# Block-causal attention and SwiGLU on one core: float64 weights unpacked with fewer instructions, keys turned in place, a new instruction list with more filler matmuls

## The chip, the cores and the metric

The kernel runs on one core of one Trainium2 chip. The metric is the device time of one execution in microseconds (us). TensorE (PE) multiplies matrices into PSUM, VectorE (DVE) and ScalarE (ACT) work elementwise, GpSimd (POOL) takes maxima and sums over partitions here, and SyncE (SP) issues nearly all DMAs.

## What is computed

```python
def _attn_ref(q, k, v):                      # (8 batches, 8 heads, 576 positions, 64)
    scores = np.matmul(q, k.transpose(0, 1, 3, 2)) / np.sqrt(64)
    mask = block_i >= block_j                # blocks of 64 positions
    scores = np.where(mask, scores, -1e9)
    scores = scores - scores.max(-1, keepdims=True)
    attn = np.exp(scores)
    attn = attn / (attn.sum(-1, keepdims=True) + 1e-9)
    return np.matmul(attn, v)

def _moe_ref(x, w_gate, w_val, w_out):       # x: (4608, 512), from all heads; weights 512 x 1536, 1536 x 512
    g = x @ w_gate
    silu = g * (1.0 / (1.0 + np.exp(-g)))
    return (silu * (x @ w_val) @ w_out).astype(np.float32)
```

The three weight matrices arrive as float64, q, k and v as float32.

## The kernel before

**The list.** The whole kernel is written as tasks: `add(engine, cost, rank, fn, after, bufs, ...)` makes one, with an assumed cost, a rank, what it comes after and the buffers it uses. `in_order()` then plays all tasks through against their assumed costs. At each moment every engine takes, of the tasks that could run and for whose buffers there is room, the one of lowest rank. What comes out is one fixed instruction order per engine, and each engine executes its own strictly in that order. Ranks come from tables: `PIECES` and `AHEAD` (36 weight pieces), `FIRST` (attention of batches 0 and 1), `SIDE`, `LEAD`, `EAGER`. A DMA's landing is assumed as the queue's end plus 0.9 us. Times up to `SETTLED` = 215 us of that play are treated as the opening.

**Filler.** Where the play leaves PE idle for more than 0.3 us in the opening, `keep_busy` puts filler matmuls (64 columns of `ones`, result unused) in front of the next PE task: `int(gap / 0.25)` of them at the very start, `int(0.6 * gap / 0.12)` afterwards. Each filler call is two passes in the trace.

**Attention.** Heads go in pairs. For batches 0 and 1 (`plain_scores`) q and k are turned by PE (line 435), copied out of PSUM by ACT into `parts` (line 443), multiplied into `at` or `po` (line 461), copied to `sc` (479, 493); DVE takes a running maximum (729), POOL the maximum over partitions (733), DVE subtracts (757), ACT takes the exponential (761), PE multiplies by v and by `ones` (801). From batch 2 on `row_scores` turns q and k with DVE (648) and splits each into a rounded part and a rest (651, 654), so that three fp32r products (672) make up a full one. It holds the raw q and k in one buffer of the pair `qk` and the turned keys in the other.

**Weights.** Each of the 36 pieces (12 chunks of gate, val and out) is loaded as pairs of 32-bit words of a float64 (968), and made a float32: ACT writes the sign bits apart into `ob` (`signs`, 983), ACT scales the high word (`scaled`, 987), DVE shifts the low word right by 29 and ors the sign in (`fraction`, 992), DVE shifts the high word left by 3 and ors (`exponent`, 997). Then ACT rounds (`high`, 1002) and DVE takes the rest (`low`, 1005).

**Feed-forward.** Tiles of 256 tokens: `xhl` (token parts) times `g_even`, `g_odd`, `v_all` into `gv` (line 1124), tanh and products on ACT and DVE (1163 to 1179), then `hhl` times w_out into `po` (1223 to 1225). The first tiles run between the attention of batches 0 and 1, as their weights arrive; the last tiles are done in three pairs with seven products in place of eight (1498, 1619 to 1621).

The lines of the weight unpacking and of the filler before:

```python
        def signs():
            nc.scalar.mul(to, w, 2.0**-60)                     # to: 16-bit halves of y ("ob")
        def fraction():
            nc.vector.scalar_tensor_tensor(
                words_of(0), words_of(0), 29, s, ALU.logical_shift_right, ALU.bitwise_or)
    ...
        for _ in range(int(t.gap / 0.25 if t.at < 8.0 else FILL * t.gap / 0.12)):
            nc.tensor.matmul(to[0:D, 0:D], lhsT=ones, rhs=ones, start=True, stop=True)
```

Of the kernel before, what the change touches and what calls it, by code (L numbers as in the profile page):

```python
# [10 lines left out]
F16 = mybir.dt.float16  # L11
# [7 lines left out]
def kernel(  # L19
# [33 lines left out]
    LEAD, EAGER = 1.69311, 0.3  # L53
# [5 lines left out]
    ROWS = (2, 3, 4, 5, 6, 7)  # L59
# [4 lines left out]
    AHEAD = {(0, 1): 2.01, (0, 2): 2.07, (1, 0): 2.03, (1, 1): 2.5, (1, 2): 2.5}  # L64
    LATER = 0.6

    PIECES = [
        (2.46498, 1.85126, 2.0295),
        (4.86232, 5.94853, 3.63137),
        (4.59615, 2.52017, 1.48427),  # L70
        (3.86967, 3.05824, 5.34888),
        (1.93206, 3.59139, 2.41171),
        (5.13877, 6.90631, 5.83015),
        (3.57653, 2.93377, 2.93471),
        (0.0797053, 1.36382, 0.915695),
        (-2.09572, -5.85789, -4.34371),
        (-7.47749, -5.87222, -3.82425),
        (-7.64215, -9.14061, -8.44419),
        (-12.1092, -9.50108, -10.8836),
    ]  # L80

    SIDE = (2.97811, 4.18833)

    PATIENCE = 10.0
    FILL = 0.6

    FIRST = {
        0: [(0, 256, (-4.21445, 2.40818, 2.05548, 2.12375)), (256, 576, (-2.9124, -2.06995, -6.61901, -4.10645))],
        1: [(0, 256, (4.0214, 3.93624, 4.15916, 3.63076)), (256, 576, (-2.93177, 1.89587, 2.55533, 4.50202))],
# [5 lines left out]
    SETTLED = 215.0  # L95
# [97 lines left out]

    unseen = const.tile([P, 1], F32, name="unseen")
# [55 lines left out]
    def chunks_of_zero(KHL):  # L250
        nc.gpsimd.memset(KHL[:, :, S:SP].bitcast(F32), 0.0)

    def zeros(x):
        def fill(QL, KS):
            nc.vector.memset(KS[:, S:SP].bitcast(F32), 0.0)
            nc.vector.memset(QL[own(1 - x)].bitcast(F32), 0.0)

        return fill

# [7 lines left out]
        high=([([P, 2, QKW], F32R)], None),  # L267
        keys=([([P, 2, QKW], F32R)], chunks_of_zero),
# [14 lines left out]
        low0=([([P, S], F32R), ([P, SP], F32R)], zeros(0)),  # L283
        low1=([([P, S], F32R), ([P, SP], F32R)], zeros(1)),
# [8 lines left out]

    pool_of(
        const,
        "ob",
        2,
        out=([([P, DM], F32)], None),
        signs=([([P, DM, 2], F16)], lambda t: nc.gpsimd.memset(t.bitcast(F32), 0.0)),
    )  # L300
    pool_of(
        const,
        "wo",
        5,
        raw=([([P, (1 + wide) * DM], I32 if wide else F32)], None),
# [216 lines left out]

# [1342 lines left out]
```

## Time and profile before

| | us |
|---|---|
| median of 3 runs (1148.54 to 1151.68) | 1150.09 |
| the profiled execution, its own time | 1151.43 |
| its span, first to last instruction | 1149.7 |
| PE busy in the span | 1127.7 |
| DVE / ACT / POOL busy | 888.5 / 605.4 / 320.9 |

"Busy" is the time in which at least one instruction of the engine was under way. The span less PE's busy time is what PE spent idle. A filler matmul counts as busy.

### The profile page before, as it was taken

The page shows a single profiled execution, that of the slowest core. Times are in us where ns is not written, and L with a number is a line of the kernel's source. Part 1 is how long each engine was busy: PE and PEld are TensorE (multiplying, and loading weights), DVE is VectorE, ACT ScalarE, POOL GpSimd, SP SyncE. Part 2 cuts the span into 40 slices and gives each one's busy share as a digit, 9 for nine tenths or more (in the row PEclk, how much of TensorE's full clock was granted, in tenths as well). Part 3 has the DMA queues.
Part 4 walks back from the last instruction along what each step waited for, and adds up shares of the span by engine and source line. Part 5 has one row for each costly group of instructions (what it writes and reads, how often), then busy time and mean ns, then how long its engine had stood idle before and what let it go on. Part 6 is the DMA issues. An engine that isn't in the chain of part 4 may idle for free.

```text
span 1149.7 us, 22749 instructions
## 1 busy us (share of the span) xinstructions
PE 1127.7 (98%) x8728; PEld 995.9 (87%) x8728; DVE 888.5 (77%) x1526; ACT 605.4 (53%) x1126; POOL 320.9 (28%) x139
## 2 busy tenths in 40 slices
PE   7999999999999999999999999999999999999998
PEld 5677778898899898888888889888999999999997
DVE  5899898687787889989899898888753855656554
ACT  5888777565554555455565555455422433334323
POOL 3213111036643543334434535444320000000000
PEclk9999999999999999999999999999999999999999
DMA  8767757676665767876786758673468867767761
GB/s 196 192 183 186 204 167 267 171 210 182 167 158 147 203 178 206 225 220 173 206 224 186 207 159 246 175 205 119 167 235 259 272 217 235 236 229 247 234 201 69
DMA packets 294445, 228.92 MB, mean 199 GB/s; under 512 B 196608, under 2 KB 245008, under 8 KB 294336
## 3 DMA queue, kind: packets, MB, share of 16 engines
q1 hardware_dynamic: 291760, 226.75, 67.3%
q8 instruction: 68, 1.11, 0.4%
q10 hardware_dynamic: 2576, 0.72, 0.3%
q14 instruction: 41, 0.34, 0.1%
HBM read 190.45 MB, written 36.96 MB: 198 GB/s over the span
## 4 chain that ended last, share of the span: by engine, by line
PE 84%; DMA 5%; DVE 4%; ACT 4%; SPq 1%; issue 1%; POOL 0%; DVEq 0%; POOLq 0%; ACTq 0%
PE gv L1124 31%; PE gv L1498 15%; PE at L801 6%; PE at L672 6%; PE po L1223 5%; PE po L1224 5%; PE po L1225 5%; PE po L1620 1%; PE po L1619 1%; PE at L1621 1%; PE po L1621 1%; PE at L1620 1%; PE at L1619 1%; DMA wo<-in_moe_w_val_dram 1%; DMA wo<-in_moe_w_gate_dram 1%
## 5 line engine op out<-in xcount | busy, mean ns | idle before, releaser
L852 POOL PARTITION_ALL_REDUCE mx<-mx x48 | 180.1, 3799 | 212.0 <-DVE mx L729 153.8
L733 POOL PARTITION_ALL_REDUCE mx<-mx x80 | 138.3, 1778 | 309.6 <-DVE mx L729 218.9
L1124 PE MATMUL gv<-xhl,v_all 128*128 128x256 f32 x1728 | 219.3, 279 | 1.7 <-DVE v_all L1005 1.1
L1124 PEld LDWEIGHTS gv<-xhl,v_all 128*128 128x128 f32 x1728 | 206.5, 188 | 7.4 <-issue 2.8
L757 DVE TENSOR_TENSOR sc<-sc,mx 128x640 f32<-128x640 f32 (+6 forms) x168 | 123.6, 774 | 16.4 <-POOL mx L733 16.4
L761 ACT ACTIVATE sc<-sc 128x1024 f32<-128x1024 f32 (+3 forms) x104 | 106.2, 1032 | 48.0 <-DVE sc L757 47.4
L1124 PE MATMUL gv<-xhl,g_even 128*128 128x256 f32 x864 | 117.9, 281 | 0.0
L1124 PE MATMUL gv<-xhl,g_odd 128*128 128x256 f32 x864 | 116.9, 282 | 0.0
L1124 PEld LDWEIGHTS gv<-xhl,g_even 128*128 128x128 f32 x864 | 110.8, 188 | 6.9 <-issue 1.9
L729 DVE TENSOR_TENSOR mx<-mx,sc 128x128 f32<-128x128 f32 (+2 forms) x180 | 110.9, 619 | 2.1 <-ACT sc L493 0.4
L1124 PEld LDWEIGHTS gv<-xhl,g_odd 128*128 128x128 f32 x864 | 106.2, 188 | 5.1 <-issue 2.6
L1223 PE MATMUL po<-wo,hhl 128*128 128x512 f32 x252 | 101.6, 403 | 0.0
L1224 PE MATMUL po<-wo,hhl 128*128 128x512 f32 x252 | 98.7, 392 | 0.0
L1225 PE MATMUL po<-wo,hhl 128*128 128x512 f32 x252 | 98.3, 390 | 0.0
L801 PE MATMUL at<-sc,v 128*64 128x128 f32 (+4 forms) x848 | 90.0, 361 | 2.2 <-ACT parts L443 1.4
L689 ACT ACTIVATE sc<-at 128x576 f32<-128x576 f32 (+1 forms) x96 | 75.8, 835 | 27.7 <-PE at L672 27.6
L1176 ACT CAST hhl<-t 128x512 fp32r<-128x512 f32 x72 | 44.7, 621 | 82.8 <-DVE t L1171 70.8
L801 PEld LDWEIGHTS at<-sc,v 128*64 128x64 f32 x848 | 56.0, 137 | 35.8 <-ACT parts L443 1.6
L1179 DVE TENSOR_TENSOR hhl<-t,hhl 128x512 fp32r<-128x512 f32 x72 | 71.3, 990 | 17.2 <-ACT hhl L1176 17.2
L729 DVE TENSOR_TENSOR mx<-sc 128x896 f32<-128x896 f32 (+2 forms) x68 | 70.0, 1031 | 7.4 <-ACT sc L701 3.9
L672 PE MATMUL at<-parts,qk 64*128 64x288 f32 (+4 forms) x864 | 73.3, 310 | 0.7 <-ACT sc L689 0.7
L672 PEld LDWEIGHTS at<-parts,qk 64*128 64x128 f32 x864 | 62.0, 185 | 9.6 <-issue 1.1
(223 smaller groups left out, 2041.2 us busy)
## 6 DMA issues: line engine op xcount, KB each, us to landing
wo<-wo_d SPq DMA_DIRECT2D x164, 512.0 KB
v_all<-sum_d SPq DMA_DIRECT2D x36, 512.0 KB
v_all<-sum_d SPq DMA_DIRECT2D x72, 256.0 KB
sum_d<-wo SPq DMA_DIRECT2D x48, 256.0 KB
v<-in_v_dram SPq DMA_DIRECT2D x64, 128.0 KB
qk<-in_q_dram SPq DMA_DIRECT2D x112, 72.0 KB
out_dram<-ob SPq DMA_DIRECT2D x30, 256.0 KB
qk<-in_k_dram SPq DMA_DIRECT2D x104, 72.0 KB
```

The source lines that it names most:

```text
L672: nc.tensor.matmul(ps[0][:, x, o : o + w], lhsT=part(1, kl)[own(x), c * P : (c + 1) * P], rhs=part(0, ql)[own(x), qs : qs + w], start=n == ...
L729: nc.vector.tensor_tensor(into, prev, of(c), op)
L733: nc.gpsimd.partition_all_reduce(m, m, channels=P, reduce_op=bass_isa.ReduceOp.max)
L757: nc.vector.tensor_tensor(piece(c), scores_of(c), m, ALU.subtract)
L761: nc.scalar.activation(x, x, AF.Exp)
L801: nc.tensor.matmul(ps[0][own(x), 1 - i if sums else i, q0 - s0 : s1 - s0], lhsT=ones if sums else vt[0][:, 2 * lane + c, own(x)], rhs=sc[0 ...
L852: nc.gpsimd.partition_all_reduce(m, m, channels=P, reduce_op=bass_isa.ReduceOp.add)
L1124: nc.tensor.matmul(o, lhsT=hilo[a][:, d], rhs=xs[d][1][b][:, 0:w], start=ds[0] == 0 and n == 0, stop=ds[-1] == NDC - 1 and n == len(trio) - 1,
L1223: nc.tensor.matmul(po, lhsT=hi, rhs=whi, start=i + y == 0, stop=False)
L1224: nc.tensor.matmul(po, lhsT=hi, rhs=wlo, start=False, stop=False)
L1225: nc.tensor.matmul(po, lhsT=lo, rhs=whi, start=False, stop=i + y == NFC - 1)
L1498: nc.tensor.matmul(ps[0][:, half * XT : (half + 1) * XT], lhsT=stationary(a, j, s), rhs=part(o, j, m), start=begin and k == 0, stop=all(a ...
```

## The change

The source calls shrink, and nearly every table number changes; so does the place of most instructions.

- **Weights.** `signs` is gone. The sign now comes out of `scaled`, which uses `Prelu` with a slope that gives negative words another factor. `fraction` no longer ors a sign in: for the 18 pieces listed in `SHIFTED` it is a DVE shift with one input (line 876), for the other 18 an ACT instruction that reads the top byte of the low word and scales it (line 874, its bias from the tile `floor`). `ob` is no longer used for signs.
- **q and k.** Raw q and k lie in the same `qk` buffer that later takes the turned keys, so a pair of heads holds one of the two buffers, not both. The key's rounding waits for both turns. ACT now writes 64 columns of zeros behind the keys per half for each pair of heads (24 more instructions from batch 2 on); POOL wrote them once.
- **The list.** DMAs that are issued between 8 and 60 us of the play are assumed to land 1.2 or 1.5 us later. After 215 us an `at` buffer is taken as free 0.8 us later and an attention task on PE as ready 0.8 us later. All ranks are new.
- **Filler.** `FILL * gap / 0.12` with 0.6 becomes `FILL * gap / 0.06` with 0.8. The program holds 226 filler calls, 96 before; the first two groups (13 and 6) stay.
- An unused variant of the scores (`split_scores`) is deleted.

```diff
-    LEAD, EAGER = 1.69311, 0.3
+    LEAD, EAGER = 5.982852, 22.492407
...
-    AHEAD = {(0, 1): 2.01, (0, 2): 2.07, (1, 0): 2.03, (1, 1): 2.5, (1, 2): 2.5}
+    AHEAD = {(0, 1): 18.047719, (0, 2): 4.730354, (1, 0): -3.813423, (1, 1): 4.489137, (1, 2): -6.161143}
...
+    SHIFTED = ((0, 0), (1, 0), (1, 1), (1, 2), (2, 0), (3, 0), (3, 1), (3, 2), (4, 0), (4, 1), (6, 2), (7, 0), (8, 0), (8, 2), (9, 0), (9, 1), (10, 0), (10, 2))
...
-    FILL = 0.6
+    FILL = 0.8
...
+    EARLY = 60.0
+    SETTLED, MARGIN = 215.0, 0.8
...
-        def signs():
-            w = words_of(1).bitcast(F32)
-            to = y[0].rearrange("p (n m) t -> p n m t", n=parts)[:, :, :, 1]
-            nc.scalar.mul(to, w, 2.0**-60)
 
         def scaled():
             w = words_of(1).bitcast(F32)
-            nc.scalar.mul(w, w, 2.0**-112)
+            nc.scalar.activation(w, w, AF.Prelu, scale=2.0**-112, alpha=-(2.0**32))
+        by_act = (i, kind) not in SHIFTED
 
         def fraction():
-            s = y[0].rearrange("p m t -> p (m t)").bitcast(I32).rearrange("p (n m) -> p n m", n=parts)
-            nc.vector.scalar_tensor_tensor(
-                words_of(0), words_of(0), 29, s, ALU.logical_shift_right, ALU.bitwise_or
-            )
+            if by_act:
+                tops = raw[0].bitcast(U8).rearrange("p (n t) -> p n t", t=8)[:, :, 3]
+                tops = tops.rearrange("p (n m) -> p n m", n=parts)
+                nc.scalar.activation(words_of(0), tops, AF.Identity, scale=1.0 / 32, bias=floor)
+                return
+            nc.vector.tensor_scalar(words_of(0), words_of(0), 29, None, ALU.logical_shift_right)
...
+                    if i:
+                        nc.scalar.mul(keys[0][:, :, S:SP], zeros, 0.0)
...
                 if t.moves:
                     queue = max(queue, end + 0.65) + t.moves
                     done = queue + 0.9 + t.more
+                    if 8.0 < now < EARLY:
+                        done += 1.2 if t.moves < 1.2 else 1.5
...
-                    u.free_at = max(u.free_at, done)
+                    u.free_at = max(u.free_at, done + (MARGIN if u.tag == "at" and now > SETTLED else 0.0))
...
-        for _ in range(int(t.gap / 0.25 if t.at < 8.0 else FILL * t.gap / 0.12)):
+        for _ in range(int(t.gap / 0.25 if t.at < 8.0 else FILL * t.gap / 0.06)):
```

Three places show how the list moved. The first is on ACT, where the second weight piece (`wo_0_109`, of w_val) stands among the copies of the turned q and k out of PSUM. Before:

```order
L443 ACTIVATE parts_1_90<-gv_0_175 128x288
L1002 CAST g_even_75<-wo_0_108 128x4x128
L983 ACTIVATE ob_0_84<-wo_0_109 128x512
L987 ACTIVATE wo_0_109<-wo_0_109 128x512
L761 ACTIVATE sc_0_243<-sc_0_243 128x2x384
L443 ACTIVATE parts_1_87<-at_0_203 128x576
L355 CAST xhl_0_92<-xt_0_311 128x256
```

and now:

```order
L647 ACTIVATE sc_0_245<-sc_0_245 128x2x384
L427 ACTIVATE parts_0_86<-at_0_199 128x384
L874 ACTIVATE wo_0_109<-wo_0_109,floor 128x512
L427 ACTIVATE parts_1_87<-at_0_199 128x576
L866 ACTIVATE wo_0_109<-wo_0_109 128x512
L339 CAST xhl_0_92<-xt_0_305 128x256
```

Before, three instructions stood between the arrival of the weight and the copy of 576 columns (983, 987, 761); now one does (874), and the exponential has moved ahead of it.

The second is on PE, at the scores of the second tile of batch 0 (line 461 before, 445 now; lines 1836 and 1720 are the filler). Before:

```order
L461 MATMUL at_0_203<-parts_0_89,parts_1_90 128x320 x2
L461 MATMUL at_0_203<-parts_0_89,parts_1_90 128x192 x2
L1836 MATMUL gv_0_175<-ones 64x64 x8
L461 MATMUL at_0_203<-parts_0_89,parts_1_90 128x320 x2
L461 MATMUL at_0_203<-parts_0_89,parts_1_90 128x64 x2
L1836 MATMUL gv_0_175<-ones 64x64 x6
L461 MATMUL at_0_155<-parts_0_89,parts_1_90 128x320 x2
```

and now:

```order
L1720 MATMUL gv_0_175<-ones 64x64 x11
L445 MATMUL at_0_155<-parts_0_89,parts_1_90 128x320 x2
L445 MATMUL at_0_155<-parts_0_89,parts_1_90 128x192 x2
L1720 MATMUL gv_0_175<-ones 64x64 x25
L445 MATMUL at_0_155<-parts_0_89,parts_1_90 128x320 x2
L445 MATMUL at_0_155<-parts_0_89,parts_1_90 128x64 x2
L1720 MATMUL gv_0_175<-ones 64x64 x13
L445 MATMUL at_0_199<-parts_0_89,parts_1_90 128x320 x2
```

The products are the same; 14 filler calls between and after them became 38, and 11 stand ahead.

The third is further on in PE's order, ahead of a product with v (line 801 before, 687 now). Before:

```order
L1836 MATMUL gv_0_169<-ones 64x64 x8
L461 MATMUL at_0_203<-parts_0_89,parts_1_90 128x320 x2
L435 MATMUL po_0_238<-ident,qk_0_146 128x96 x3
L1836 MATMUL gv_0_169<-ones 64x64 x6
L801 MATMUL at_0_155<-sc_0_243,v_0_78 64x320 x6
```

and now:

```order
L1008 MATMUL gv_0_175<-xhl_0_98,v_all_75 128x256
L1008 MATMUL gv_0_175<-xhl_1_99,v_all_75 128x256
L1008 MATMUL gv_0_175<-xhl_0_98,v_all_76 128x256
L1720 MATMUL po_0_250<-ones 64x64 x50
L687 MATMUL at_0_199<-sc_0_377,v_0_82 64x320 x6
L687 MATMUL at_0_199<-sc_0_377,v_0_82 64x192 x2
```

One group of 50 filler calls stands where two of 8 and 6 stood; feed-forward matmuls (line 1008) come right before it.

## Rows read from the trace of the kernel before

**Rows 1.** From the page: the span, and each engine's busy time, share of the span and instructions.

```profile
span 1149.7 us, 22749 instructions
PE 1127.7 (98%) x8728; PEld 995.9 (87%) x8728; DVE 888.5 (77%) x1526; ACT 605.4 (53%) x1126; POOL 320.9 (28%) x139
```

**Rows 2.** The span by stages: from and to, length, then busy time (and instructions) of PE, its weight loads, DVE, ACT and POOL; the granted TensorE clock (1.00 is 2.4 GHz, 0.50 is 1.2), the DMA engines' busy share, GB/s.

```profile
0.00:28.00 28.00, 19.78 (x192) 16.31 (x192) 15.49 (x46) 16.10 (x34) 8.86 (x16) 0.94 0.82 199
28.00:71.00 43.00, 39.05 (x372) 28.79 (x372) 39.19 (x79) 37.39 (x70) 11.12 (x8) 1.00 0.63 167
71.00:130.00 59.00, 56.21 (x455) 44.89 (x452) 53.14 (x95) 49.18 (x97) 14.92 (x12) 1.00 0.77 208
130.00:220.00 90.00, 88.37 (x626) 72.81 (x626) 75.38 (x128) 63.02 (x109) 8.44 (x7) 1.00 0.67 200
220.00:400.00 180.00, 179.63 (x1439) 158.48 (x1438) 144.09 (x218) 100.57 (x174) 81.45 (x29) 1.00 0.66 177
400.00:800.00 400.00, 399.32 (x3188) 355.04 (x3186) 356.74 (x588) 214.00 (x373) 177.80 (x62) 1.00 0.70 198
800.00:1144.00 344.00, 344.00 (x2463) 318.84 (x2464) 204.04 (x378) 123.14 (x272) 18.25 (x6) 1.00 0.65 215
1144.00:1150.00 6.00, 1.31 (x6) 0.75 (x4) 0.42 (x1) 2.02 (x4) 0.00 (x0) 0.78 0.48 175
```

**Rows 3.** What PE waited for in the whole span, costliest first: us in total, times, longest.

```profile
PE at L461 <- ACT parts L443: 4.1, 3, 3.1
PE at L461 <- ACT sc L493: 1.8, 3, 0.9
PE at L435 <- DMA qk<-in_q_dram: 1.5, 1, 1.5
PE at L801 <- ACT parts L443: 1.4, 1, 1.4
PE gv L1124 <- DVE v_all L1005: 1.1, 1, 1.1
PE at L1836 <- DVE ones L192: 1.0, 1, 1.0
...
PE at L672 <- ACT sc L689: 0.7, 1, 0.7
...
PE gv L435 <- DVE ident L335: 0.4, 1, 0.4
```

**Rows 4.** The filler matmuls (line 1836): durations (ns, least, median, most) and count of passes by the PSUM tile they write; then PE's time in two stretches that each hold one group of filler.

```profile
L1836 PE MATMUL gv<-ones x136: 219/222/369, 15.9 to 70.2; 128*64 128x64 f32 x136
L1836 PE MATMUL at<-ones x56: 222/270/368, 1.0 to 13.4; 128*64 128x64 f32 x56
...
12.90:13.70 0.80, 0.68 (x8) 0.54 (x8) 1.00 0.55 123
30.90:32.30 1.40, 1.26 (x18) 1.12 (x18) 1.00 0.55 215
```

**Rows 5.** PE in order of time around its longest wait (start, length, what, idle before and its releaser), and the stretch in which the granted clock was lower (columns as in rows 2).

```profile
18.64 0.71 PE L435 MATMUL at<-ident,qk 96*128 96x96 f32 x6 [0.18 <-DVE sc L757]
19.29 0.80 PE L1836 MATMUL gv<-ones 128*64 128x64 f32 x10
23.20 0.92 PE L461 MATMUL at<-parts,parts 64*128 64x256 f32 x8 [3.12 <-ACT parts L443]
...
24.40:27.80 3.40, 3.40 (x24) 2.29 (x21) 2.13 (x6) 2.77 (x6) 0.00 (x0) 0.50 0.80 226
```

**Rows 6.** ACT in order of time in the same stretch.

```profile
20.40 0.78 ACT L983 ACTIVATE ob<-wo 128x512 f16<-128x512 f32 x1 [3.33 <-DMA wo<-in_moe_w_val_dram]
21.21 0.68 ACT L987 ACTIVATE wo<-wo 128x512 f32<-128x512 f32 x1
21.79 0.83 ACT L761 ACTIVATE sc<-sc 128x768 f32<-128x768 f32 x1
22.52 0.63 ACT L443 ACTIVATE parts<-at 128x576 f32<-128x576 f32 x1
```

**Rows 7.** Groups of ACT and DVE instructions by line and shape: count, busy us, mean ns of one, idle before them and its releasers.

```profile
L983 ACT ACTIVATE ob<-wo 128x512 f16<-128x512 f32 x36 | 28.7, 801 | 11.5 <-DMA wo<-in_moe_w_gate_dram 5.1 <-DMA wo<-in_moe_w_val_dram 5.1 <-DMA wo<-in_moe_w_out_dram 1.2
L987 ACT ACTIVATE wo<-wo 128x512 f32<-128x512 f32 x36 | 24.6, 692 | 0.3
L701 ACT ACTIVATE sc<-at,unseen 128x128 f32<-128x128 f32 x24 | 8.9, 370 | 0.0
L992 DVE SCALAR_TENSOR_TENSOR wo<-wo,ob 128x512 int32<-128x512 int32 x36 | 26.5, 740 | 4.6 <-ACT ob L983 4.5
L335 DVE TENSOR_SCALAR ident<-t 128x128 f32<-128x128 f32 x1 | 0.3, 286 | 0.0
L648 DVE STREAM_TRANSPOSE sr<-qk 128x576 f32<-128x576 f32 x48 | 35.5, 760 | 0.8 <-DMA qk<-in_q_dram 0.8
```

**Rows 8.** POOL's maxima over partitions of the opening and the longest of the DVE shifts: a group as in rows 7, and least, median and most ns.

```profile
L733 POOL PARTITION_ALL_REDUCE mx<-mx x80 | 138.3, 1778 | 309.6 <-DVE mx L729 218.9 <-issue 48.6 <-ACT wo L1292 12.9
L992 DVE SCALAR_TENSOR_TENSOR wo<-wo,ob x36: 678/693/1123, 13.1 to 201.9; 128x512 int32<-128x512 int32 x36
```

**Rows 9.** The feed-forward matmuls of line 1124 alone in two stages: length, PE busy time with these and their count, the weight loads', clock, DMA share, GB/s.

```profile
71.00:220.00 149.00, 73.75 (x537) 66.89 (x538) 1.00 0.71 203
400.00:800.00 400.00, 216.46 (x1776) 210.04 (x1776) 1.00 0.70 198
```

More of the change, by code (lines that the diff above doesn't have):

```diff
@@ L291 @@
     pool_of(const, "xu", 2, [([P, S], F32)])
[L294 to L299, printed above, removed]
-    )
+    pool_of(const, "ob", 2, out=([([P, DM], F32)], None))
     pool_of(
@@ L619, in first_max @@
-            def first_max():
-                nc.scalar.copy(mx[0][:, :, 0:P], sc[0][:, :, 0:P])
-            evac[0].append(add("ACT", act_us(2 * P), Q, first_max, evac[0], [sc, mx]))
-        def row_scores():
-            raw, keys = qk
-            def load(i):
-                for x, hd in enumerate(heads):
-                    for j in range(D // 32):
-                        rows = slice(x * D + 32 * j, x * D + 32 * (j + 1))
-                        nc.sync.dma_start(
-                            out=raw[0][rows, i, 0:S].rearrange("p (n d) -> p n d", d=32),
+                            out=raw(i)[rows].rearrange("p (n d) -> p n d", d=32),
@@ L656, in low_part @@
                     )
[L658 to L660 removed]
+                ld = dma(R, 3e5, lambda i=i: load(i), [], [keys], 4, packet=128)
+                turns.append(add("DVE", dve_us(S), R, turn, [ld], [turned, keys]))
+                t = add("ACT", act_us(S) + 0.2 * i, R, high_part, turns[:], [turned, to])
                 ready.append(add("DVE", dve_us(S), R, low_part, [t], [turned, to], True))
@@ L1009, in weight @@
         if wide:
-            t = add("ACT", act_us(DM, more=0.13), R, signs, [t], [raw, y])
-            f = add("DVE", dve_us(DM), R, fraction, [t], [raw, y], True)
+            if by_act:
+                f = add("ACT", act_us(DM, more=0.17), R, fraction, [t], [raw])
+            else:
+                f = add("DVE", 0.07 + 0.00077 * DM, R, fraction, [t], [raw])
             t = add("ACT", act_us(DM, more=0.06), R, scaled, [t], [raw])
@@ L1808, in in_order @@
                     x.waits -= 1
-                    x.ready = max(x.ready, end if x.engine == e == "PE" or x.behind is t else done)
+                    then = end if x.engine == e == "PE" or x.behind is t else done
+                    if x.mode and e != "PE" and now > SETTLED:
+                        then += MARGIN
+                    x.ready = max(x.ready, then)
                     if not x.waits:
```

147 lines of the change are left out of this document (30 added, 117 removed).

## The prediction, made before the changed kernel ran

> **What bounds the kernel now.** I read the page's busy times first [rows 1]: PE is busy 1127.7 of 1149.7 us, so all other engines together can cost at most the 22.0 us that PE is idle, and no engine that is merely busy matters. Next the stages [rows 2], where a stage's length less PE's busy time is its idle time: 8.2 us in 0 to 28, 4.0 in 28 to 71, 2.8 in 71 to 130, 1.6 in 130 to 220, 0.4 and 0.7 up to 800, none from there to 1144, 4.4 in the last stretch, which ends at 1149.7. So from 220 on PE runs through, and a new order can win 1.1 us there; the last 400 rows of PE's order are the same in both programs, and the end keeps its 4.4 us. What can change lies in the opening, 16.6 us of idle time.
>
> That time has two companions which the busy figure hides. One is the filler. 96 calls make 192 passes [rows 4]. A group of 8 passes takes 0.68 us and one of 18 takes 1.26, so one more pass costs (1.26 - 0.68) / 10 = 0.058 us and a call 0.116. The rest of a group, some 0.16 us, is the drain of its last pass (222 ns long), which the next matmul overlaps unless it has to wait. All filler lies before 70.2 us. The other is the clock: from 24.4 to 27.8 us the granted clock is 0.50, which is 1.2 GHz, and before it PE had idled 3.12 us [rows 5]. 3.4 us at half speed are 1.7 us lost.
>
> What ended the idle time [rows 3] is mostly ACT: copies of the turned q and k (line 443) and of the scores (493). The longest wait, 3.1 us, can be followed: ACT stood 3.33 us before line 983 until a weight had landed at 20.40, then did 983, 987 and an exponential (0.78, 0.68 and 0.83 us), and only then the copy PE's order was held by, which ended at 23.15 [rows 6]. DVE is 91% busy from 28 to 71 and 90% from 71 to 130, ACT 87% and 83% [rows 2].
>
> "Busy" could hide further waits: a matmul of line 1124 takes 73.75 / 537 = 137 ns of PE's busy time each from 71 to 220, and 216.46 / 1776 = 122 ns from 400 to 800 [rows 9]. If all of the difference were waiting, that would be 537 x 15 ns = 8.1 us; most of it must be the shorter runs of that stage, at whose ends a drain shows, so I put it into the lower bound alone. The Trainium skill (Perfetto Trace Analysis, Identifying the Most-Contended Engine) warns that matmul busy time is a poor measure of how near PE is to its limit, because matmuls are pipelined. The trace bears that out only as far as these 15 ns; by the rule taken at its word the opening would hold up to 8.1 us more than its idle time shows.
>
> **The change, part by part.**
>
> *Filler.* 226 calls in place of 96: 130 x 0.116 = +15.1 us of PE time, wherever they stand. By place: 79 for 45 up to the first feed-forward matmuls (+3.9 us, the stage 0 to 28), 137 for 51 up to the group of 50 (+10.0, the stage 28 to 71), 10 for none later (+1.2). Filler is free only where PE would have waited anyway. In 28 to 71 PE lost 51 x 0.116 + 4.0 = 9.9 us to filler and idling together, and now 137 x 0.116 = 15.9 us of filler alone stand there. So PE has hardly any wait left there, and the filler itself sets the pace.
>
> *Order in 0 to 28.* The list now assumes later landings, and ACT has one weight instruction between the landing and the copy of 576 columns. With 0.8 us for it and 0.63 for the copy, the copy ends near 20.40 + 0.8 + 0.65 = 21.9, against 23.15. In front of PE's next product stand 11 filler calls (1.3 us), where the group before had 5 (0.6). So the 3.1 us fall below 1, and with no such pause I expect no stretch at half clock. The start's waits for `ones` and `ident` (1.0 and 0.4) stay, and so do landings of q and k that the filler does not reach: of 8.2 us I leave 3.7. That is -4.5, -1.7 for the clock, -0.5 for three drains that are overlapped again.
>
> *28 to 71.* Idle 4.0 to 0.7 is -3.3, and six drains are -1.0.
>
> *71 to 220.* Here the weights count. `signs` goes: ACT -28.7 us. 18 fractions on ACT cost between 0.69 and 0.80 us by the nearest rows of the same width (987 and 983) [rows 7]; I take 0.8, since they read a bias and bytes with a stride: +14.4, net -14.3. On DVE 36 shifts of 0.74 us go and 18 with one input come. Their price lies between 0.29 (line 335, a quarter of the width) and 0.74; I take 0.5, +9.0, net -17.5 us [rows 7]. `Prelu` needs no further table: the order holds one table load before and after. This relief is off PE's path except where PE waits for ACT or DVE, and from 71 to 220 that is 4.4 us in short waits (line 443 1.4, line 1005 1.1). DVE at about 85% and ACT at 75% there lose about a tenth of their work. I leave 1.2 of the 4.4: -3.2.
>
> *From 220 on.* The margins make the list leave more room before an attention product: of 1.1 us perhaps half, -0.6. The 24 zero writes cost at most 0.37 us each (line 701 on 128 columns [rows 7]), 8.9 us of ACT, which is busy 214 of 400 us there: nothing. Without that cover each would delay a key's rounding by 0.37. Sharing the `qk` buffer makes a load wait for the products of the pair two before, no longer for its turns; DVE waited 0.8 us in all for these loads [rows 7]. I price it at 0, at most 2 us if several loads come late.
>
> **The sum.** +15.1 (filler) - 1.7 (clock) - 4.5 - 0.5 (0 to 28) - 3.3 - 1.0 (28 to 71) - 3.2 (71 to 220) - 0.6 = +0.3 us. The profiled execution took 1151.43 us with a span of 1149.7; the median shown, 1150.09, lies 1.3 below it, and I add the difference to the median: 1150.4 us. Filler for 1.3% of the time is bought, and waiting for as much is sold. About 0.3%, 3.5 us, is what a measurement of this kernel can tell from no change.
>
> **Rivals.**
>
> *The waits go altogether (faster).* What I left beside the start's 1.4 us is 2.3 in 0 to 28, 0.7, 1.2 and 0.5, together 4.7; without it 1145.7, and with a part of the hidden 8.1 us about 1145. For it: DVE and ACT are so full in 28 to 130 that a tenth less work shortens every queue. Against it: landings don't move, and in 28 to 71 filler sets the pace, so that earlier data win nothing. It decides once PE idles under 2.5 us in all before the last stretch, the start included.
>
> *The filler pushes the chain (slower).* A group stands ahead of a product whose scores ACT, DVE and POOL must pass on before PE can go on. A group that is longer than the wait delays that product, and so the next wait's end too: the wait after it is as long as before, with filler in front. For it: the 38 calls between the scores of one pair of heads are 4.4 us, and the 50 are 5.8, where 14 and 14 (1.6 each) stood with waits under 1 us. Then only half of the 12.2 us of idle time in 0 to 71 goes in place of 7.8, and the waits from 71 on stay: 1150.4 + 1.7 + 3.2 = 1155.3. It decides once over 8 us of idle time stay before 71, or over 4 from 71 to 220.
>
> *DVE's shift meets POOL (slower).* The list keeps two-input shifts out of POOL's spans but not the new one-input shift. Before, the longest of line 992 took 1.12 us for a median of 0.69, and POOL's maxima last 1.78 [rows 8]. If the new shift waits out a maximum, each meeting costs up to 1.8 us of DVE, and with POOL busy 23 of 149 us from 71 to 220 [rows 2] some three of 18 meet one: about 5 us of DVE, and the 4.4 us of PE's waits stay: 1150.4 + 3.2 = 1153.6. The Trainium skill (SBUF - State Buffer, SBUF: two separate sides) says that a DVE instruction in a two-port mode and a GpSimd instruction lock each other out for their whole length. The rows show stretched shifts, no clean lock, so I give it little.
>
> **Chances.** My forecast, within 0.3%: 0.50. The waits go: 0.24. The filler pushes the chain: 0.22. The shift meets POOL: 0.04. So faster 0.24, same 0.50, slower 0.26. The range must hold 8 in 10 and reach toward both signs: 1144.8, just below the second case, to 1155.2, just short of the third. My own case alone runs from 1147.5 to 1153, by 1 us on what stays in 0 to 28, 1 in 71 to 220, and 0.29 or 0.74 for the shift, which is 4 us of DVE and hardly one of PE.
>
> **What would show it.** In the profile after: 452 filler passes at 0.058 us; PE idle near 4 us in 0 to 28 and under 1.5 in 28 to 71, with more busy time there by 10 us of filler; no stretch at clock 0.50 before the end; the wait of 3.1 us at the first tile's product gone; DVE's weight work lower by 17 us and ACT's by 14; waits from 71 to 220 near 1 us; the feed-forward of the second tile no earlier than now. I am wrong if the filler's passes don't run at this price, if idle time past 71 grows under the new order, or if from 220 on PE no longer runs through.

## The result, and the profile after

The changed kernel takes 1164.1 us (median of 5 runs, 1162.58 to 1166.24), against 1150.09 before: a ratio of 1.0121, with a 95% interval from 1.0104 to 1.0138. I had said 1150.4, with 1144.8 to 1155.2 as the range, and put 0.26 on slower.

The profiled execution of the change has a span of 1164.1 us (its own time is 1166.24). Each trace here is of one execution, which can lie up to 3.9 us off the median of its kernel. From the page, the busy times that answer to [rows 1]:

```profile
PE 1141.6 (98%) x8988; PEld 1012.5 (87%) x8988; DVE 879.2 (76%) x1509; ACT 597.2 (51%) x1132; POOL 324.2 (28%) x136
```

PE is idle for 22.5 us, as before (22.0). It is busy for 13.9 us more. By stages, as in [rows 2] (length, then busy time of PE, PEld, DVE, ACT, POOL; granted clock, DMA share, GB/s):

```profile
0.00:28.00 28.00, 25.21 (x289) 21.98 (x291) 16.02 (x50) 16.57 (x34) 10.54 (x16) 1.00 0.88 192
28.00:71.00 43.00, 43.00 (x502) 36.13 (x502) 34.41 (x66) 31.53 (x58) 7.84 (x6) 1.00 0.69 173
71.00:130.00 59.00, 55.87 (x479) 45.41 (x475) 50.55 (x94) 49.04 (x98) 15.87 (x12) 1.00 0.70 192
130.00:220.00 90.00, 86.01 (x611) 72.80 (x608) 64.40 (x112) 54.75 (x94) 9.90 (x6) 1.00 0.73 210
220.00:400.00 180.00, 180.00 (x1432) 158.38 (x1430) 138.01 (x223) 102.00 (x184) 74.10 (x26) 1.00 0.65 177
400.00:800.00 400.00, 391.75 (x3125) 344.68 (x3124) 370.51 (x590) 221.76 (x398) 187.67 (x64) 1.00 0.70 190
800.00:1144.00 344.00, 344.00 (x2467) 319.23 (x2467) 196.25 (x359) 114.73 (x255) 18.24 (x6) 1.00 0.68 224
```

A stage's length less PE's busy time is its idle time. Beside what I had forecast:

| stage, us | idle before | forecast | idle after |
|---|---|---|---|
| 0 to 28 | 8.2 | 3.7 | 2.8 |
| 28 to 71 | 4.0 | 0.7 | 0.0 |
| 71 to 220 | 4.4 | 1.2 | 7.1 |
| 220 to 400 | 0.4 | } 0.5 | 0.0 |
| 400 to 800 | 0.7 | } (220 to 1144) | 8.3 |
| 800 to 1144 | 0.0 | } | 0.0 |

So the opening gave up its waiting, even a little more than I said, and as much waiting turned up later. From 400 to 800, where PE had run through, it now waits at these places (what PE waited for in that stage: us in total, times, longest):

```profile
PE gv L1008 <- DVE t L1050: 3.3, 2, 2.1
PE po L1107 <- DMA wo<-wo_d: 1.9, 1, 1.9
PE at L558 <- ACT xu L702: 1.9, 2, 1.3
PE at L558 <- ACT sc L575: 1.2, 2, 1.0
```

The longest can be followed. DVE in order of time around 583 us (start, length, instruction, idle before it and its releaser):

```profile
582.96 0.42 DVE L968 TENSOR_TENSOR xt<-xt,rt 128x256 f32<-128x256 f32 x1 [3.24 <-DMA v<-in_v_dram]
583.30 0.55 DVE L615 TENSOR_TENSOR mx<-mx,sc 128x384 f32<-128x384 f32 x1
583.77 1.35 DVE L643 TENSOR_TENSOR sc<-sc,mx 128x1152 f32<-128x1152 f32 x1
585.04 0.68 DVE L1050 SCALAR_TENSOR_TENSOR t<-t,gv 128x512 f32<-128x512 f32 x1
```

And PE in the same stretch:

```profile
583.25 0.39 PE L1109 MATMUL po<-wo,hhl 128*128 128x512 f32 x1
585.77 1.68 PE L1008 MATMUL gv<-xhl,g_even 128*128 128x256 f32 x12 [2.13 <-DVE t L1050]
588.46 1.75 PE L558 MATMUL at<-parts,qk 64*128 64x448 f32 x20 [1.00 <-ACT sc L575]
```

DVE stood 3.24 us in front of the product of x with the inverse sums, for a coming tile, because a load had not landed. The trace names one of v; the product itself reads `rt`, whose loads SP had issued only then (SP's queue):

```profile
579.40 1.49 SPq L962 DMA_DIRECT2D rt<-r_d  x2
```

Behind it in DVE's fixed order stood the instruction that frees the `gv` buffer PE needs (line 1050). It ended at 585.72, and PE went on at 585.77. Near 734 PE itself waits 1.92 us for a load of output weights, and the clock then drops (PE in order of time, then the stretch at the lower clock with the columns of [rows 2]).

```profile
734.19 0.50 PE L1107 MATMUL po<-wo,hhl 128*128 128x512 f32 x1 [1.92 <-DMA wo<-wo_d]
...
735.10:738.50 3.40, 3.40 (x15) 3.11 (x14) 3.40 (x3) 0.06 (x1) 3.40 (x2) 0.50 0.52 138
```

That is 1.2 GHz for 3.4 us, 1.7 us lost, as much as the stretch of [rows 5] cost. That earlier stretch is gone, as forecast.

### The profile page after: what moved, and what is told of

Same layout as the page of the kernel before. It is cut to its first block, busy times and chain, and to the rows that moved or that the text cites. A ratio compares the mean times of both kernels' runs of the same rounds, so it can differ in the third digit from the quotient of the medians.

```text
span 1164.1 us, 23267 instructions
## 1 busy us (share of the span) xinstructions
PE 1141.6 (98%) x8988; PEld 1012.5 (87%) x8988; DVE 879.2 (76%) x1509; ACT 597.2 (51%) x1132; POOL 324.2 (28%) x136
## 4 chain that ended last, share of the span: by engine, by line
PE 80%; DMA 7%; DVE 6%; ACT 3%; SPq 2%; issue 1%; POOL 1%; DVEq 0%; POOLq 0%
PE gv L1008 27%; PE gv L1382 15%; PE at L687 6%; PE at L558 5%; PE po L1107 5%; PE po L1109 4%; PE po L1108 4%; DMA wo<-wo_d 1%; PE po L1504 1%; PE po L1503 1%; PE at L1505 1%; PE po L1505 1%; PE at L1504 1%; PE at L1503 1%; DVE mx L615 1%
## 5 line engine op out<-in xcount | busy, mean ns | idle before, releaser
L619 POOL PARTITION_ALL_REDUCE mx<-mx x80 | 142.7, 1833 | 353.2 <-DVE mx L615 142.0
L738 POOL PARTITION_ALL_REDUCE mx<-mx x48 | 180.1, 3798 | 154.2 <-DVE mx L615 128.5
L1008 PE MATMUL gv<-xhl,v_all 128*128 128x256 f32 x1728 | 222.6, 280 | 0.0
L643 DVE TENSOR_TENSOR sc<-sc,mx 128x640 f32<-128x640 f32 (+6 forms) x168 | 136.5, 843 | 3.4 <-POOL mx L619 3.4
L687 PE MATMUL at<-sc,v 128*64 128x320 f32 (+4 forms) x820 | 86.5, 360 | 1.5 <-ACT sc L477 1.1
L615 DVE TENSOR_TENSOR mx<-sc 128x896 f32<-128x896 f32 (+2 forms) x68 | 73.3, 1081 | 12.1 <-ACT sc L587 9.3
L1063 DVE TENSOR_TENSOR hhl<-t,hhl 128x512 fp32r<-128x512 f32 x72 | 63.0, 875 | 22.6 <-ACT hhl L1060 22.4
L1055 DVE SCALAR_TENSOR_TENSOR t<-t,gv 128x512 f32<-128x512 f32 x72 | 49.0, 681 | 38.5 <-PE gv L1008 37.9
```

The costliest lines, as they stand in the source:

```text
L615: nc.vector.tensor_tensor(into, prev, of(c), op)
L619: nc.gpsimd.partition_all_reduce(m, m, channels=P, reduce_op=bass_isa.ReduceOp.max)
L643: nc.vector.tensor_tensor(piece(c), scores_of(c), m, ALU.subtract)
L687: nc.tensor.matmul(ps[0][own(x), 1 - i if sums else i, q0 - s0 : s1 - s0], lhsT=ones if sums else vt[0][:, 2 * lane + c, own(x)], rhs=sc[0 ...
L738: nc.gpsimd.partition_all_reduce(m, m, channels=P, reduce_op=bass_isa.ReduceOp.add)
L1008: nc.tensor.matmul(o, lhsT=hilo[a][:, d], rhs=xs[d][1][b][:, 0:w], start=ds[0] == 0 and n == 0, stop=ds[-1] == NDC - 1 and n == len(trio) - 1,
```

## The experiments

**1. The filler: is it paid for?** Two runs exchange the filler rules between the kernels; all other instructions keep their order.

```diff
 e1_old_filler (the changed kernel)        e2_new_filler (the kernel before): the reverse
-    FILL = 0.8
+    FILL = 0.6
-        ... else FILL * t.gap / 0.06)):
+        ... else FILL * t.gap / 0.12)):
```

> The changed kernel with the filler rule of before (0.6 of the planned gap in calls of two passes of 0.06, as before); the order of all other work is the changed one, instruction for instruction. Theory A (the new filler is paid nearly in full, since PE ran through from 8 to 71 us in the changed kernel): the stage up to 71 us gets shorter by 7 to 12 us, of the 15 us of filler that go some 3 to 8 come back as waiting, and the median is 1152 to 1157. Rival B (the filler lay in waits that the new order has anyway; the loss lies behind 71 us in the order): filler goes and waiting of the same size comes, the median is 1161 to 1165. Both expect the 8 us of idle time from 400 to 800 to stay within 2 us, since no filler stands there.

> The kernel before with the filler rule of the change alone (0.8 of the planned gap); the order of all other work is that of before. Theory A: PE's busy time grows by the added passes at 0.058 us each and idle time up to 71 us, 12.2 us before, falls by 3 to 7 us at most; the median is 1154 to 1161. Rival B: the added passes lie in waits that are there, the median stays within 1148 to 1152.

Measured: the changed kernel with the old filler 1159.02 us, 0.81% over the kernel before (0.60 to 1.02), so the new filler costs it about 0.40% (1.21 less 0.81), some 4.6 us; the two intervals together leave 0.1 to 0.7%. The kernel before with the new filler: 1156.72 us, 0.62% over (0.41 to 0.82).

The first lies between theory and rival. Filler time falls from 31.4 to 16.1 us and idle time up to 71 us rises from 2.8 to 8.3, both as A said, and the 7.9 us of idle time from 400 to 800 stay. But its profile shows 10.2 us at half clock, where the changed kernel has 3.4:

```profile
581.80:585.20 3.40, 3.12 (x19) 2.71 (x17) 2.92 (x3) 2.73 (x6) 3.40 (x2) 0.50 0.55 207
151.70:158.50 6.80, 6.39 (x28) 5.46 (x29) 2.77 (x5) 2.97 (x6) 0.00 (x0) 0.50 0.77 167
```

So without the added filler a part of what it costs is lost again to the clock. The second has A's time, but its idle time up to 71 us falls by 10.5 us, more than A's 7. In its profile PE's filler time grows from 16.5 to 33.7 us, and the idle time of the whole span falls from 22.0 to 10.9. So some two thirds of the added passes took the place of waiting and of the half clock; the rest is a loss. From 28 to 71 us PE is then busy for all 43.00 us, as in the changed kernel. In the opening of the changed kernel filler even stands ahead of work that is ready:

```profile
19.95 0.79 ACT L874 ACTIVATE wo<-wo,floor 128x512 int32<-128x512 uint8 x1 [0.68 <-DMA wo<-in_moe_w_val_dram]
20.63 0.63 ACT L427 ACTIVATE parts<-at 128x576 f32<-128x576 f32 x1
```

```profile
20.50 1.50 PE L1720 MATMUL gv<-ones 128*64 128x64 f32 x22
21.93 0.92 PE L445 MATMUL po<-parts,parts 64*128 64x256 f32 x8
```

The copy that PE's product had waited for [rows 5, 6] ends at 21.26; the 22 passes of filler before the product end only at 21.9.

**2. Code or tables?** One run keeps the changed code and takes the tables and rules of before (ranks, no later landings, `MARGIN = 0`, old filler). The other keeps the code of before and takes the new tables, landings and margins.

```diff
 e3_old_tables: the changed code
-    LEAD, EAGER = 5.982852, 22.492407
+    LEAD, EAGER = 1.69311, 0.3
...
-    EARLY = 60.0
-    SETTLED, MARGIN = 215.0, 0.8
+    EARLY = 0.0
+    SETTLED, MARGIN = 215.0, 0.0
```

> The changed code (bytes, scaling for the sign, raw q and k in the buffer of the turned keys, zero writes) with the tables of ranks and the rules of before (no later landings, no margin, filler rule of before). Theory C (the 8.2 us of idle time from 400 to 800 and the 7 from 71 to 220 come with the order that the new ranks give): idle time from 400 to 800 is 2 us or less, and the median is 1146 to 1153. Rival D (they come with the shared buffer, whose loads land later): 5 us or more of idle time from 400 to 800, behind waits for a load of q or k, and the median is 1154 to 1160.

> The code of before (three weight instructions with two inputs, own buffers for raw q and k, no zero writes) with the new tables of ranks, later landings, margin, and the filler rule of before. Theory C (the order of the new ranks makes the idle time behind 71 us): 5 us or more idle from 400 to 800, median 1155 to 1162. Rival D (the shared buffer makes it): 2 us or less idle from 400 to 800, median 1148 to 1154.

Measured: changed code, old tables 1158.97 us (0.85% over, 0.61 to 1.09), with 5.4 us idle from 400 to 800. Old code, new tables 1183.37 us (2.91% over, 2.67 to 3.15), with 12.2 us idle from 220 to 400 and 3.3 from 400 to 800. The first has the numbers of theory D, but not its waits: none of PE's waits from 400 to 800 stands behind a load of q or k (us in total, times, longest).

```profile
PE gv L1008 <- DVE t L1050: 3.7, 5, 1.3
PE at L558 <- ACT xu L702: 1.1, 1, 1.1
PE at L558 <- ACT sc L575: 0.4, 1, 0.4
```

DVE itself waited 5.1 us for such loads there, and whether that reaches PE is open. The second fits neither theory. So the new tables alone don't make these stalls, and the old ones don't take them away. My reading is that tables and code go together, since the ranks were found for the tasks that they stand with.

**3. Each half of the code alone, and a control.** f1 is the kernel before with only the shared buffer for raw q, k and keys; f2 with only the new weight instructions; g1 moves one rank by 0.01.

```diff
 f1_shared_buffer
-                        bufs = [(Buf("qk", "raw"), Buf("qk", "keys")), Buf("parts", "queries")]
+                        bufs = [Buf("qk", "keys"), Buf("parts", "queries")]
...
 f2_new_weights
-            nc.scalar.mul(w, w, 2.0**-112)
+            nc.scalar.activation(w, w, AF.Prelu, scale=2.0**-112, alpha=-(2.0**32))
...
 g1_rank_nudged
-    LEAD, EAGER = 1.69311, 0.3
+    LEAD, EAGER = 1.68, 0.3
```

> The kernel before with one part of the change alone: raw q and k land in the buffer of the turned keys, with the zero writes on ACT and the planner's price for them; weights, tables, rules and filler as before. Theory C1 (sharing the buffer brings the idle time from 220 on, since the loads of q and k and the work behind them land at other times and POOL and DVE meet more): 4 us or more of idle time from 400 to 800 and a median 5 to 11 us above the kernel before. Rival C2 (the weights' new instructions bring it, through the list): under 2 us of idle time there and a median within 3.5 us of the kernel before. Rival C3 (any changed list loses about as much, since the order before stands at numbers that fit it alone): 4 to 11 us above in this run and in the next two alike.

> The kernel before with the other part alone: the weights' bytes by ACT, the one-input shift by DVE, the sign by scaling, no sign buffer; q, k, tables, rules and filler as before. My prediction's weight relief (ACT 14 and DVE 17.5 us less) would by itself win up to 3 us. C1: median 1 to 4 us below the kernel before, idle time from 400 to 800 as before, since no weight is unpacked there. C2 and C3: 4 us or more of idle time from 400 to 800 and a median 4 to 11 us above.

> Control: the kernel before with one number of the list changed by 0.01 (the rank of the late attention pieces, LEAD 1.68 in place of 1.69311); every instruction is the same, only the order shifts in places. C3: 4 us or more above the kernel before, and more overlap of DVE with POOL from 400 to 800. C1 and C2: within 3.5 us of the kernel before.

Measured: f1 1152.09 us (0.29% over, 0.15 to 0.43), f2 1157.81 (0.80%, 0.61 to 1.00), g1 1153.83 (0.37%, 0.22 to 0.52). A rank that moves by 0.01 costs as much as the whole shared buffer, so what f1 loses can't be put down to the buffer: C1 falls. C2 fits f1, but it falls with f2, which idles 0.0 us from 400 to 800, and with g1, which was to stay within 3.5 us and loses 4.3. C3 has the sizes roughly right (f1, at 3.3 us, lies below its 4 us, g1 just above), though not the place, which was to be this stage, and in g1 DVE runs less beside POOL from 400 to 800, not more (125 us against 142, the time in which both are busy, added up from the traces). Where f1 and g1 lose their time isn't shown: their profiled executions are 1.2 and 2.5 us faster than their medians, with 18.6 and 20.2 us of idle time in all, less than the 22.0 of the kernel before. f2, which by my weight term should have been faster, is the slowest of the three. Its profiled execution has 20.6 us of idle time in all, less than before, but two waits of 2.5 and 2.8 us, each with a stretch at half clock behind it:

```profile
22.70:29.50 6.80, 6.80 (x39) 5.03 (x41) 2.75 (x6) 5.20 (x11) 1.86 (x2) 0.50 0.75 179
872.60:876.00 3.40, 3.40 (x16) 3.22 (x17) 1.71 (x6) 0.55 (x2) 0.00 (x0) 0.51 0.98 365
```

That is 5.1 us lost to the clock, where the kernel before lost 1.7. Its new order also gets more filler by the old rule, 224 passes for 192, some 1.9 us. From 71 to 220 us, where DVE is busy 15 us less (113.5 for 128.5), PE's idle time falls from 4.4 to 3.3 us only. In f2 the last weight is unpacked near 188 us, so the wait near 872 comes with the order; the same wait of 2.8 us stands in the run with the old code and the new tables.

f1 also speaks against a cause I had in mind for the stalls. In the changed kernel DVE is busy for 370.5 us from 400 to 800, against 356.7 [rows 2], and for more of that time POOL is busy too (166 us for 142, added up from the traces). In f1 DVE is just as busy, 164 us of it beside POOL, and PE hardly waits:

```profile
400.00:800.00 400.00, 399.53 (x3187) 353.64 (x3186) 370.76 (x602) 221.61 (x399) 189.38 (x65) 1.00 0.68 193
```

**4. One waiting instruction.** In the changed kernel with the old filler, DVE's product near 578 us that stood 3.2 us before a load is put behind the feed-forward instruction that PE waited for. In g2 that one instruction is moved alone; the load that reuses its buffer then stands ahead of it, so it waits for that load and multiplies by the next values. In g3 the loads that reuse its buffers move along.

```diff
 g2_divide_later
     order = in_order()
+    late = [t for t in order if t.fn.__qualname__.endswith("bring_x.<locals>.divide")][29]
+    at = order.index(late)
+    to = next(i for i in range(at, len(order)) if order[i].fn.__qualname__.endswith("silu2"))
...
+    order[at : to + 1] = [*order[at + 1 : to + 1], late]
```

> The changed kernel with the filler rule of before, and one DVE instruction (the product of x with the inverse sums near 578 us, which stood 3.2 us before a load) put three instructions further back in DVE's order, behind the first feed-forward product that PE waits for. If PE's wait of 2.2 us near 581 comes from that one instruction, it goes, and with it the 3.4 us at half clock that follow: idle time from 400 to 800 falls from 7.9 to about 5.5 us and the median by 3 to 4.5 us against the same kernel without the move (1159.0, or 0.8% over the kernel before). Rival (the engines behind are late anyway, the wait only moves): idle time there stays above 7, the median stays within 1.5 us.

> The changed kernel with the filler rule of before, and the one DVE instruction that stood 3.2 us before a load near 578 us (x times the inverse sums) put three instructions further back in DVE's order, together with the loads that reuse its buffers; all else as it was. If PE's wait of 2.2 us near 581 hangs on that one instruction, it goes with the 3.4 us at half clock behind it: the idle time from 400 to 800 falls from 7.9 to about 5.5 us and the median to 0.4 to 0.6% over the kernel before, from 0.81%. Rival (the work behind is late anyway): idle time there stays above 7 us, the median stays at 0.7 to 0.9%.

Measured: g2 1160.52 us (1.02% over, 0.82 to 1.22), g3 1155.22 (0.55%, 0.36 to 0.75), against 0.81% without the move. In g2 DVE waits twice as long, and PE with it:

```profile
582.03 0.43 DVE L968 TENSOR_TENSOR xt<-xt,rt 128x256 f32<-128x256 f32 x1 [6.71 <-DMA rt<-r_d]
```

```profile
585.19 2.40 PE L558 MATMUL at<-parts,qk 64*128 64x448 f32 x14 [6.93 <-ACT sc L575]
```

So one DVE instruction that waits for a load does reach PE: 6.71 us there, 6.93 here. In g3 DVE waits 0.20 us, and PE's wait for line 1050 is gone there, but in the same round it waits 1.83 us for ACT's copy (line 575), 0.28 before, and 3.4 us at half clock follow as before. The product, which took 0.43 us, now stands beside a sum over partitions on POOL and takes 1.87:

```profile
572.73 1.87 DVE L968 TENSOR_TENSOR xt<-xt,rt 128x256 f32<-128x256 f32 x1 [0.20 <-DMA v<-in_v_dram]
```

```profile
570.82 8.13 POOL L738 PARTITION_ALL_REDUCE mx<-mx  x2 [1.50 <-DVE mx L615]
```

DVE's turn of a key (line 532) comes right behind it, and ACT's copy behind that, so these 1.44 us are most of the wait that is left. Idle time from 400 to 800 is 6.6 us, between the two expectations; the time is the one forecast for the case that the wait hangs on that instruction. But the gain of 0.26% comes with intervals that overlap, and a part of it lies near 150 us, where the run without the move had 6.8 us at half clock; I don't count it as shown.

**5. The margin, and how far lists scatter.** Four runs change only `MARGIN`, which acts from 215 us on, in the changed kernel with the old filler; e1 above is the same at 0.8.

```diff
 h1_margin_075 (h3: 0.7, h4: 0.85, e5: 0.0)
-    SETTLED, MARGIN = 215.0, 0.8
+    SETTLED, MARGIN = 215.0, 0.75
```

> Control on the changed side: the changed kernel with the filler rule of before and the margin 0.75 in place of 0.8, nothing else; the order differs in places from 215 us on. Theory L (what a list wins or loses behind 220 us is scatter, since the list knows nothing of what makes an instruction late): idle time from 400 to 800, 7.9 us without the nudge, moves by 2 us or more, and the waits stand at other instructions. Rival (the stalls belong to the changed work, whatever the order): 7 to 9 us, at the same instructions.

> The changed kernel with the filler rule of before and no margin (0 for 0.8). Theory M (the margins make the stalls, since they hold instructions back that could run): 2 us or less idle from 400 to 800, median 0.1 to 0.4% over the kernel before. Rival (the margins help, or do nothing): 6 us or more, median 0.7% over or more. Theory L: anything from 2 to 12 us.

> The changed kernel with the filler rule of before and the margin 0.7. Theory L (scatter): anything from 0 to 0.9% over the kernel before, with idle time from 400 to 800 between 1 and 9 us at other instructions than at 0.75 or 0.8. Rival (a smaller margin is better in itself): under 0.28%; but no margin at all gave 0.79%, so I hold this for unlikely.

> The changed kernel with the filler rule of before and the margin 0.85. Theory L: as for 0.7, 0 to 0.9%. If 0.7 and 0.85 both lie at 0.7% or more, 0.75 was a lucky draw; if both lie under 0.4%, 0.8 was an unlucky one.

| margin | over the kernel before (interval), % | idle 400 to 800, us | first product of line 558 to the end, us |
|---|---|---|---|
| 0 | 0.79 (0.58 to 1.01) | 3.7 | 932.8 |
| 0.7 | 0.24 (0.10 to 0.38) | 2.5 | 924.5 |
| 0.75 | 0.28 (0.15 to 0.41) | 3.3 | 925.6 |
| 0.8 | 0.81 (0.60 to 1.02) | 7.9 | 932.0 |
| 0.85 | 0.28 (0.18 to 0.37) | 3.6 | 927.4 |

The last column is the span less the start of the first scores of batch 2 and later; the changed kernel itself, with the new filler, takes 931.5 us there. So three neighbours of the chosen margin are 0.5% faster than it, and the chosen one is no better than none. That 0.7 lies under 0.28% is what its rival asked for, but no margin at all gives 0.79% and 0.85 does as well as 0.75: a smaller margin is not better in itself. The two columns of trace numbers are of one execution each. For 0.75 the waits of that stage are (compare the list of the changed kernel above):

```profile
PE at L558 <- ACT xu L702: 2.1, 1, 2.1
PE po L1107 <- ACT ob L1137: 0.7, 1, 0.7
PE po L1107 <- DMA wo<-wo_d: 0.2, 1, 0.2
PE at L558 <- ACT sc L575: 0.2, 1, 0.2
```

The stalls stand elsewhere, and the long ones behind line 1050 and the output weights are gone.

**6. Both together, and no filler at all.**

```diff
 h2_margin_075_new_filler: the changed kernel
-    SETTLED, MARGIN = 215.0, 0.8
+    SETTLED, MARGIN = 215.0, 0.75
...
 k1_no_filler: the kernel before (k2: the changed kernel with margin 0.75)
-    FILL = 0.6
+    FILL = 0.0
```

> The changed kernel whole, with its own filler rule, and the margin 0.75 in place of 0.8. If the two losses are separate and add up (filler in the opening, the list behind 71 us): 0.28% for this list with the old filler plus 0.40 for the filler (1.21 less 0.81), so 0.6 to 0.8% over the kernel before. Rival (the filler delays the chain and so makes the later stalls worse, or better): 1.0% or more, or 0.4% or less.

> The kernel before without any filler behind the first 8 us (some 146 passes less), same order. If filler is paid for about half, as the two runs with more of it say: PE's filler time falls by 8 to 10 us, 4 to 6 come back as waiting, and one or two more stretches at half clock cost 1.7 each; the median is 1145 to 1149. Rival (the filler before just keeps the clock up): the clock stays at half over 10 us or more of the opening and the median is 1152 or more.

> The changed kernel with the margin 0.75 and no filler behind the first 8 us. On the side of before, no filler at all measured the same as its filler (0.13%, interval -0.02 to 0.29), since 5 us at half clock and the waits took back what the passes cost. By the same sum: within 0.2% of the same list with the old filler, so 0.1 to 0.5% over the kernel before. Rival (the weights' relief lets the opening run without filler): 0.2% or more below it, so as fast as the kernel before or faster.

Measured: h2 1159.51 us, 0.93% over (0.79 to 1.08), between adding up (0.6 to 0.8) and its rival (1.0 or more). Against 0.28% for the same list with the old filler, the new filler costs 0.65% here, more than the 0.40% at margin 0.8; and with the new filler the margin 0.8 costs 0.28% (1.21 less 0.93), less than the 0.53% with the old. These differences of 0.25% are no larger than the noise of the four intervals, so whether the two losses add up stays open. Without filler the kernel before takes 1150.55 us (0.13% over, -0.02 to 0.29), the changed one with 0.75 takes 1153.43 (0.39%, 0.20 to 0.58, against 0.28 with the old filler). Both show no difference from the old filler. In the first, filler time falls from 16.5 to 4.6 us, and 13.6 us of the opening run at half clock:

```profile
16.70:20.10 3.40, 3.40 (x22) 2.45 (x18) 1.92 (x5) 2.62 (x4) 3.31 (x4) 0.50 1.16 258
27.00:33.80 6.80, 5.96 (x31) 4.50 (x28) 6.56 (x11) 5.58 (x10) 2.48 (x2) 0.50 0.34 126
44.00:47.40 3.40, 3.31 (x14) 1.83 (x16) 3.40 (x8) 2.61 (x6) 0.00 (x0) 0.50 0.92 235
```

Half of that time, 6.8 us, is lost, 5.1 us more than the kernel before loses. The rival's 10 us at half clock came, its time of 1152 us didn't; the theory's 1145 to 1149 didn't either. I had expected 4 to 6 us to come back as waiting, but the idle time of this profile is 22.4 us against 22.0. It is an execution 2.1 us faster than the median; over the 12 executions the mean clock of the span is 0.986 to 0.994 (0.997 to 1.000 in the kernel before), and the two slowest have 0.986 and 0.990. So more half clock takes back a part of what the passes cost; the rest isn't shown. No version that I ran beats the kernel before.

## Why the prediction was wrong

The sum gave +0.3 us. In the spans the difference is +14.4 (1164.1 less 1149.7). In the sum's own terms it is filler +14.9, idle time up to 71 us -9.4, from 71 to 220 +2.7, from 220 to 1144 +7.2, and -1.0 in the rest of PE's busy time; at half clock 1.7 us went and 1.7 came.

- **Filler, +15.1: right.** 452 passes, 31.39 us of PE's time against 16.48, +14.9, so 0.057 us a pass. The places are a little off: +5.4, +7.9 and +1.6 us in the three stages, where I had 3.9, 10.0 and 1.2.
- **0 to 28 and 28 to 71, together -7.8 idle, no half clock: right, and short by 1.6.** Idle time fell by 9.4. The long wait and the slow stretch went. The copy ended at 21.26, forecast 21.9. For the drains I had -1.5; their price of 0.16 us was too low by my own rows (0.68 less 8 x 0.058 is 0.22), and the trace doesn't show them apart from the 1.0 above. So the balance of the opening, +15.1 - 1.7 - 4.5 - 0.5 - 3.3 - 1.0 = +4.1, was about right, even a little high (14.9 - 1.7 - 9.4 = +3.8 before the drains). What I did not draw from it is that the wait had been traded for filler at a poor rate: the exchange of the rules, by itself, costs 0.40, 0.62 and 0.65% in three pairs, some 4.6 to 7.5 us.
- **71 to 220, -3.2: the first step that failed.** It came out at +2.7. The size of the relief was right: ACT's byte fractions took 774 ns each (0.8 forecast), DVE's one-input shift 480 ns (0.5), and 15.0 and 17.9 us of work went, as forecast. But the step from there to PE's waits was only argued: "a tenth less work" should have shortened the queues. With the weights alone (f2) the waits of this stage fall by 1.1 us; with the changed list, whose order up to 215 us is the same in all its runs of parts 1 and 4 to 6, they are 3.9 to 7.2 us, and with the changed code and the old tables 4.4. In the changed kernel DVE is 77% and ACT 70% busy there, less than before, and PE waits for single instructions (us in total, times, longest; the four costliest):

```profile
PE at L445 <- ACT sc L477: 1.6, 2, 1.0
PE gv L1008 <- DVE t L1050: 1.3, 1, 1.3
PE at L1720 <- ACT sr L763: 1.2, 1, 1.2
PE at L687 <- ACT sc L477: 1.1, 1, 1.1
```

Nor were the 15 ns that a matmul took longer there than from 400 to 800 [rows 9] a reserve: of the 8.1 us that I had held possible, little came out. The Trainium skill's warning (Perfetto Trace Analysis, Identifying the Most-Contended Engine) that matmul busy time is a poor measure of how near PE is to its limit gave no more here than that. After the change the same two rows (length; busy time of line 1008 with the count; clock, DMA share, GB/s) give 133 and 124 ns:

```profile
71.00:220.00 149.00, 70.32 (x527) 1.00 0.71 203
400.00:800.00 400.00, 207.07 (x1669) 1.00 0.70 190
```

- **From 220 on, -0.6: the step that failed most.** It came out at +7.2, off by 7.8. I read "PE runs through" in [rows 2] as a property of the stage, and so of any list of the same work. It is one of that list. Six profiles with the old tables and at most one half of the new code idle 0 to 1.0 us from 400 to 800; the whole changed code idles 2.5 to 8.3 us under each of six orders (five margins, and the old tables). From the first scores of batch 2 to the end, without the last 4.3 us, the two groups meet: 0.7 to 3.4 us and 3.2 to 8.6. I had set the margins down as room in front of a product; they moved the order, and 0.8 was a poor draw: 0.53% against 0.75 with the old filler, 0.28% with the new. The 1.7 us of half clock near 735 stand behind one of these waits. Both signs of being wrong that I had written down for these stages came: idle time past 71 grew, and PE no longer ran through from 220 on.
- **Shared buffer and zero writes, 0: not contradicted.** f1 costs no more than a rank moved by 0.01. A zero write takes 0.31 us (0.37 at most, I had said); near 587 us in the changed kernel, and in g3, one stands just before the copy PE waits for.
- **The rivals.** "The waits go altogether" would have wanted under 2.5 us idle before the last stretch; it was 18.2. "The filler pushes the chain" has the right sign, and its bound for 71 to 220 (over 4) was passed, but its mechanism, waits that stay before 71, did not come. Six of the 18 one-input shifts ran wholly or in part beside POOL: three took 429 to 434 ns, hardly more than those away from it (419 to 432), and three 623, 686 and 918. The mean of 480 against the median of 430 is 0.9 us in all, so that rival cost next to nothing. The rule of the Trainium skill that I had set beside it (SBUF - State Buffer, SBUF: two separate sides: a DVE instruction in a two-port mode and a GpSimd instruction lock each other out for their whole length) is not shown by these shifts; whether they run in such a mode, no run tells. That any new order loses where the old one runs through stood in the text as a way to be wrong, without a chance or a time of its own. It should have been a rival: the nudge of one rank by 0.01 costs 0.37%.

Put together: the 1.21% can be taken apart in two orders. First the filler, then the margin: 0.40 and 0.53. First the margin, then the filler: 0.28 and 0.65. Both leave 0.28, the changed code and list at margin 0.75 with the old filler; the other better margins, the shared buffer and a nudged rank lose about as much against the list of before (0.24 to 0.37). That this rest is the price of leaving a well-chosen list is my reading; no run shows it, and the changed code's 2.5 us or more of idle time from 400 to 800 under every margin may hold a part of its own, such as an interplay of its two halves.

## What to carry to other kernels

A stage in which the bounding engine never waits, in a program with a fixed order, says that this order fits, not that the stage has slack: when the order changes, price the loss of that fit (here 0.24 to 0.8%) before any gain, and measure a nudge of one number as the control. Filler costs time as soon as it stands ahead of work that is ready; try none of it and half of it before more of it. Less work on other engines counts only where the chain of waits shows that this work is what ends last.

## What the runs showed of the hardware that I had not expected

A wait of 1.92 us on PE was followed by 3.4 us at 1.2 GHz in the middle of a stage that was 98% busy (near 735 us), and the 2.8 us wait of f2 near 872 likewise, while PE's 2.13 us wait at 585 us in the changed kernel was not; the same wait in e1 (2.24 us at 581) was. So in these runs a single wait of about 2 us cost nothing more, or 1.7 us more. And a DVE product took 1.87 us beside a sum over partitions on POOL (g3), 0.43 in e1 and g2, while three of six shifts beside POOL were not longer at all. Keeping PE busy with filler through the opening won nothing: without it 13.6 us ran at half clock, and the time was the same as with the 12 us of passes that prevent most of it.
